# A new order table, a division by exponentials in the first slabs, and a shorter range check placed late, in a linear attention and feed-forward kernel

## The chip, the cores and the metric

The kernel runs on one NeuronCore of a Trainium2 chip. Its engines are TensorE (PE in the profile; PEld is its loading of weights), VectorE (DVE), ScalarE (ACT), GpSimd (POOL) and SyncE (SP, which here only issues DMAs). The metric is the device time of one execution in microseconds (us): three runs of the kernel before gave 621.87, 622.42 and 624.62, median 622.42.

## The reference

Inputs are q, k, v and a complex decay a = a_re + i a_im for 4 batches, 8 heads, 768 time steps and head size 48. The decay is scaled so that its magnitude is at most 0.999. Then the state of each head, a 48 x 48 complex matrix, runs through time, and the result goes into a gated feed-forward layer (384 to 1536 to 384) over 3072 tokens:

```python
for t in range(S):
    new_re = ar * S_re - ai * S_im
    new_im = ar * S_im + ai * S_re
    S_re, S_im = new_re + kv, new_im          # kv = outer(k[t], v[t])
    y[:, :, t] = einsum('bhd,bhde->bhe', q[:, :, t], S_re)
g = x @ w_gate; val = x @ w_val               # x is y with the heads side by side
out = (g / (1 + exp(-g)) * val) @ w_out
```

The weights come as 64-bit floats.

## The kernel before

**The work.** Time is cut into 6 chunks of 128 steps, so 4 batches give 24 slabs (n = 0 to 23) of 128 steps by 8 heads. Two slabs form a group (g = 0 to 11); the names of operations end in the group, or in group.slab, or in the slab. Group 0 is prepared in two halves, 0a and 0b, which are 384 columns wide (8 heads x 48); all others are 768 wide.

**Preparation of a group** (`stage_ops`). The recurrence is replaced by running sums along time of ln|a| and of the angle of a. `ld_re`, `ld_im`, `ld_qt`, `ld_kt` load (L439). `sqr`, `sqi`, `m2` make re^2 + im^2; `lnm`, `w`, `l2` its logarithm, cut at 0.999. The angle is arctan(im/re): in group 0 `rec` is a reciprocal of re on DVE (L461) and `ratio` a product with it (L504); in the others `lnr` and `r0` make 1/re as exp(-ln re) on ACT, `e1` and `b1` multiply re and im by it on DVE and `ratio` corrects it (L506). `RCP = 1` says how many groups take the first way. `at` is the arctan. `cumL` and `cumF` are the running sums, products of PE with a triangle of ones (L541, L544). `exps` turns the first into decays; `sadd`, `rnd`, `frac`, `abs`, `cos`, `sin` turn the second into a phase, and `qtm`, `ktm`, `qs0`, `qs1`, `ks0`, `ks1` scale q and k by both. `dr1`, `dr2` send the decay of the last step through DRAM and back as the small tile `dec`, which `gm` multiplies into the state G (L400).

**A slab** (`slab_ops`). q and k are turned so that heads lie on partitions (tile T): in slabs 0 to 3 by PE (`tr`, L669, copied out by `ev`), later by DVE transposes of 32 x 32 (`tr1`, `tr0`, L689) into a lent weight tile ww, and 12 DMAs that bring the strips into place (`sh0` to `sh3`, L697). `sc` are the scores on PE, `mk` the mask on DVE (L758), `kv` the new state, `st` and `V` the values (L730, L799), `evh` and `evl` copy the result as x into a high and a low part (L817).

**Feed-forward** (`ffn_ops`), 12 steps per group: `f1_g.i` gate and value (L974), `th` Silu on ACT, `h2` the product on DVE (L985), `hh` and `hl` its high and low part, `f2_g.i` the output product (L1005). Six steps of group 0 use whole 32-bit weights (6 products for f1, 3 for f2); in all others each product is split into three of half the precision (18 and 9 products). `oe` and `os` copy out and store.

**Weights.** `wl0` load (L857), `c1` and `c3` build 32-bit floats from 64-bit ones (L869), `c4` and `c5` split them, for w_in (names end in w) and w_out (o). All weights are loaded in the first 60 us.

**Range checks.** The shortcuts hold for a range of inputs only. `kl`, `k1`, `k2` read all weights again and check them (L908, L912, L917); `ckre`, `ckim` check groups 2 to 11. `sector_ops` checks slabs 0, 6, 12 and 18, and their neighbours in groups 0 and 1: two loads, re - im and re + im on DVE (`kz0`, `kz1`), and the smallest of each (`km0`, `km1`, L941). `judge`, `tally`, `keep` (L1032 to L1044) make one count of all flags; if it is not 128, a slow general version runs.

**What sets the order.** All engines work through their own queue in order. The queues are filled from one table, `ORDER`, a list of some 2150 names, each with its engine where there is a choice (`c10w:DVE`). `Planner.plan` walks it, asserts that each name stands behind what it depends on, and puts a table load of ACT (L1103) where the next function isn't in the set that is loaded. A name's place in the list is not a time: only its place among the names of the same engine counts. `tt` (L400) and `cast` (L404, L406) are helpers, so many operations share these lines.

Of the kernel before, what the change touches and what calls it, by code (L numbers as in the profile page):

```python
# [24 lines left out]
NSLAB = B * NCH  # L25
# [9 lines left out]
RCP, SQR = 1, 2  # L35
ORDER = """
    ld_re0a ld_re0b ld_im0a ld_im0b ld_re1 ldv0 ld_im1 ldr0 wl00w wl01w ld_qt0b wl02w ld_kt0a ld_qt0a sqr0a:ACT
    sqi0a:ACT sqr0b:ACT rec0a ratio0a at0a m20a:DVE sqi0b:DVE m20b:DVE cumF0.0 lnm0a lnm0b w0a lnr1 rec0b
    sqr1:ACT sadd0.0:ACT w0b r01 l20a sqi1:DVE m21:DVE cumL0.0 exps0.0 lnm1 w1 c10w:DVE c30w ratio0b rnd0a
    frac0a:DVE c11w:DVE e11:DVE c31w abs0a at0b cumF0.1 wl04w dr10a b11:DVE ratio1 sin0a c12w:ACT cos0a l20b  # L40
    cumL0.1 at1 sadd0.1:ACT exps0.1 l21 cumL1.0 ktm0a:DVE qtm0a:DVE ks0_0a:DVE ks1_0a:DVE qs1_0a:DVE rnd0b
    frac0b:DVE qs0_0a:DVE trt010 exps1.0 wl03w ldr1 wl00o ld_kt0b ld_qt1 wl01o wl05w dr10b ldv1 dr20a trt011
    c32w c13w:DVE cumF1.0 evt010:ACT abs0b evt011:ACT trt000 trt001 sadd1.0:DVE ld_re2 ld_kt1 wl06w c33w
    evt001:DVE qtm0b:DVE c14w:DVE sin0b cumF1.1 sadd1.1:ACT evt000:ACT cumL1.1 cos0b sc0_0 sc1_0 exps1.1
    ktm0b:DVE ks0_0b:DVE ks1_0b:DVE c10o:ACT mk0_0 c34w qs1_0b:DVE qs0_0b:DVE trt110 trt111 evt110:ACT
    evt111:ACT kv0 c15w:ACT trt100 trt101 evt100:ACT evt101:ACT mk1_0 V0 dr11 wl03o dr20b wl02o wl07w fr0b
# [1235 lines left out]
```

## Time and profile before

| | us |
|---|---|
| median of 3 runs | 622.42 |
| the profiled execution | 622.05 |
| its span, first to last instruction | 620.5 |
| PE busy | 587.4 |
| PEld busy | 564.7 |
| DVE busy | 480.2 |
| ACT busy | 383.3 |
| of that, 89 table loads of ACT, 1283 ns each | 114.2 |

Busy times of engines lie beside each other. Matmuls overlap in PE's pipeline and their ends are modelled, so busy PE says little of its pace; the distance from start to start says more. A wait of an engine matters where it reaches the end. Idle time of another engine costs nothing.

### The profile page before, as it was taken

How to read it: one execution, taken by the hardware profiler on the slowest of the kernel's cores; microseconds unless marked ns; L12 is line 12 of the kernel's file. 1: busy time of each engine (PE TensorE's matmuls, PEld its weight loads, DVE VectorE, ACT ScalarE, POOL GpSimd, SP SyncE). 2: the span in 40 equal slices, each digit the busy share in tenths (PEclk: the TensorE clock that was granted, in tenths of full speed). 3: DMA queues.
4: the chain of work that ended last, by engine and by line, in shares of the span. 5: the costliest groups of instructions: out<-in, count | busy, mean ns of one | idle time of the engine just before them, and what ended most of it. 6: DMA issues, size and time to landing. Idle time of an engine off the chain costs nothing.

```text
span 620.5 us, 16959 instructions
## 1 busy us (share of the span) xinstructions
PE 587.4 (95%) x7004; PEld 564.7 (91%) x7004; DVE 480.2 (77%) x885; ACT 383.3 (62%) x668; POOL 5.6 (1%) x17
## 2 busy tenths in 40 slices
PE   2699999999989999999999999999999999999994
PEld 0378899999989999999999999999999999999994
DVE  8999999988868768978768879778766947643332
ACT  7988995864874776666857687556757365311210
POOL 3000000000000000000000000000000000000000
PEclk9999999999999999999999999999999999999999
DMA  8999125455565542664662665645571561133001
GB/s 283 334 338 306 38 48 140 119 150 157 133 173 120 133 109 54 132 161 117 135 162 73 163 157 114 162 125 117 138 173 52 130 188 52 24 101 85 28 1 30
DMA packets 154426, 81.52 MB, mean 131 GB/s; under 512 B 122715, under 2 KB 145501, under 8 KB 154342
## 3 DMA queue, kind: packets, MB, share of 16 engines
q1 hardware_dynamic: 153798, 80.11, 48.5%
q8 instruction: 57, 0.93, 0.7%
q10 hardware_dynamic: 544, 0.26, 0.1%
q14 instruction: 27, 0.22, 0.1%
HBM read 59.82 MB, written 4.78 MB: 104 GB/s over the span
## 4 chain that ended last, share of the span: by engine, by line
PE 69%; DMA 9%; DVE 7%; SPq 7%; ACT 5%; issue 3%; DVEq 0%; ACTq 0%
PE p_gv L974 36%; PE p_po L1005 18%; PE p_py L730 6%; SPq L697 5%; PE p_ps L730 5%; DMA T<-ww 2%; PE p_pm L544 2%; PE p_pm L799 2%; ACT L1103 2%; DVE ww L689 1%; DMA ww<-in_a_im_dram 1%; DMA vt<-in_v_dram 1%; DMA ww<-in_w_in_dram 1%; DMA wo<-in_w_out_dram 1%; ACT s L449 1%
## 5 line engine op out<-in xcount | busy, mean ns | idle before, releaser
L974 PE MATMUL p_gv<-xh,ww 128*128 128x256 f32 x1728 | 316.4, 282 | 1.0 <-ACT xh L817 0.6
L974 PEld LDWEIGHTS p_gv<-xh,ww 128*128 128x128 f32 x1728 | 270.9, 188 | 4.2 <-issue 1.0
L974 PE MATMUL p_gv<-xl,ww 128*128 128x256 f32 x828 | 229.6, 277 | 0.0
L974 PEld LDWEIGHTS p_gv<-xl,ww 128*128 128x128 f32 x828 | 155.5, 188 | 0.0
L1005 PE MATMUL p_po<-hh,wo 128*128 128x256 f32 x828 | 148.5, 279 | 0.0
L1005 PEld LDWEIGHTS p_po<-hh,wo 128*128 128x128 f32 x828 | 126.2, 188 | 2.4 <-issue 2.0
L980 ACT ACTIVATE sg<-p_gv 128x256 f32<-128x256 f32 x144 | 54.4, 383 | 116.6 <-PE p_gv L974 99.6
L1103 ACT ACT_TABLE_LOAD x89 | 114.2, 1283 | 1.6
L1005 PE MATMUL p_po<-hl,wo 128*128 128x256 f32 x414 | 114.8, 277 | 0.0
L985 DVE TENSOR_TENSOR sg<-sg,p_gv 128x256 f32<-128x256 f32 x144 | 59.0, 415 | 46.4 <-ACT sg L980 46.0
L1005 PEld LDWEIGHTS p_po<-hl,wo 128*128 128x128 f32 x414 | 77.7, 188 | 0.0
L400 DVE TENSOR_TENSOR hl<-sg,hh 128x256 fp32r<-128x256 f32 x138 | 57.2, 420 | 11.7 <-ACT hh L404 8.5
L449 ACT ACTIVATE s<-s 128x768 f32<-128x768 f32 x44 | 36.9, 844 | 12.0 <-DVE s L400 7.0
L758 DVE TENSOR_TENSOR sc<-p_ps,turn 128x512 f32<-128x512 f32 x48 | 32.5, 687 | 14.5 <-PE p_ps L730 14.2
L730 PEld LDWEIGHTS p_ps<-T 96*64 96x64 f32 x768 | 36.0, 138 | 7.5 <-issue 2.8
L730 PE MATMUL p_ps<-T 96*64 96x128 f32 (+1 forms) x768 | 39.5, 254 | 3.2 <-DMA T<-ww 2.4
L404 ACT CAST hh<-sg 128x256 fp32r<-128x256 f32 x56 | 22.3, 401 | 23.4 <-DVE sg L985 12.3
L406 DVE CAST hh<-sg 128x256 fp32r<-128x256 f32 x82 | 23.5, 288 | 14.9 <-PE p_po L1005 12.8
L730 PE MATMUL p_py<-sc,vr 128*32 128x128 f32 x384 | 26.0, 273 | 0.0
L730 PE MATMUL p_py<-sc,vt 128*32 128x128 f32 x384 | 25.0, 273 | 0.0
L912 DVE TENSOR_REDUCE flags<-wo 128x1 f32<-128x384 f32 x36 | 19.6, 545 | 6.9 <-DMA wo<-in_w_in_dram 6.9
L817 ACT CAST xh<-p_py 128x384 fp32r<-128x384 f32 x22 | 10.4, 474 | 22.1 <-PE p_py L730 22.1
(133 smaller groups left out, 722.7 us busy)
## 6 DMA issues: line engine op xcount, KB each, us to landing
T<-ww SPq DMA_DIRECT2D x240, 64.0 KB, 2.7
wo<-in_w_in_dram SPq DMA_DIRECT2D x24, 384.0 KB, 3.4
ww<-in_w_in_dram SPq DMA_DIRECT2D x12, 767.8 KB, 7.0
vt<-in_v_dram SPq DMA_DIRECT2D x24, 192.0 KB, 3.9
wo<-in_w_out_dram SPq DMA_DIRECT2D x12, 384.0 KB, 3.7
wo<-in_w_out_dram SPq DMA_DIRECT2D x12, 383.8 KB, 5.1
out_dram<-ost SPq DMA_DIRECT2D x34, 128.0 KB, 3.4
re<-in_a_re_dram SPq DMA_DIRECT2D x11, 384.0 KB
```

The costliest lines, as they stand in the source:

```text
L400: V[e].tensor_tensor(out=out, in0=a, in1=b, op=op)
L404: nc.scalar.copy(out=out, in_=in_)
L406: nc.vector.tensor_copy(out=out, in_=in_)
L449: nc.scalar.activation(out=of(to or dst), in_=of(source), func=func, scale=scale, **kw)
L697: nc.sync.dma_start(out=at_["T", n][32 * j:32 * j + 32].rearrange("p x (g i n) -> p (x g) i n", g=4, i=4)[:, :, i], in_=bt()[32 * i:32 * i ...
L730: nc.tensor.matmul(out=o, lhsT=l, rhs=r, start=opens, stop=closes, tile_position=(0, width * slot), skip_group_check=True)
L758: nc.vector.tensor_tensor(out=s.rearrange("p (r m) t -> p r m t", m=2), in0=scores[qd].rearrange("p (r m) t -> p r m t", m=2), in1=m, op=A ...
L974: nc.tensor.matmul(out=gv[:, i, :], lhsT=l, rhs=r, start=(m == 0), stop=(m == len(mm) - 1))
L980: nc.scalar.activation(out=new("sg", I), in_=at_["gv", I][:, 0:2 * P], func=AF.Silu)
L985: nc.vector.tensor_tensor(out=sg, in0=sg, in1=at_["gv", I][:, 2 * P:4 * P], op=ALU.mult)
L1005: nc.tensor.matmul(out=bank(j), lhsT=weight("o", f, part)[:, j * P:j * P + P], rhs=r, start=pos == 0 and m == 0 and j != 1, stop=pos == NF ...
L1103: nc.scalar.preload_act_table_set(op.load)
```

## The change

1. `RCP` goes from 1 to 0: group 0, too, gets 1/re by `lnr`, `r0`, `e1`, `b1`.
2. The range check of the first slabs takes |im| on ACT (`ka`), one difference re - |im| (`kz`) and one minimum (`km`) in place of two differences and two minima; both loads go into the tile ww, and the tile wo is not needed. Four flags become two.
3. The table `ORDER` is another one throughout.

```diff
-RCP, SQR = 1, 2
+RCP, SQR = 0, 2
 ORDER = """
-    ld_re0a ld_re0b ld_im0a ld_im0b ld_re1 ldv0 ld_im1 ldr0 wl00w wl01w ld_qt0b wl02w ld_kt0a ld_qt0a sqr0a:ACT
+    ld_im0a ld_re0a ld_im1 ld_re1 ld_im0b sqi0a:ACT lnr0a r00a sqr0a:DVE m20a:DVE e10a:DVE b10a:DVE ratio0a
...
-    NFL = 2 * NGRP + NSLAB + 6 * NF
+    NFL = 2 * NGRP - 2 + NSLAB + 6 * NF
...
-        both, parts = [(("wo", x), N) for x in range(2)], [(("ww", x), N) for x in range(2)]
+        parts = [(("ww", x), N) for x in range(2)]
+
         def at(t):
-            return spare("o") if t == "re" else spare("w")[:, A2 * (t == "z"):A2 * (t == "z") + A2]
+            return spare("w")[:, A2 * (t == "im"):A2 * (t == "im") + A2]
...
-        for i, (out_, op) in enumerate((("z", ALU.subtract), ("im", ALU.add))):
-            col = fl_re + g + NGRP * i
-
-            def both_(e, out_=out_, op=op):
-                tt(e, at(out_), at("re"), at("im"), op)
-            pl.add(f"kz{i}{N}", EITHER2, both_, deps=["klre" + N, "klim" + N] + ([f"kz0{N}"] if i else []), use=both + parts)
-
-            def least(e, out_=out_, col=col, i=i):
-                nc.vector.tensor_reduce(out=flags[:, col:col + 1], in_=at(out_), axis=AX.X, op=ALU.min)
-            pl.add(f"km{i}{N}", STT2, least, deps=[f"kz{i}{N}"], use=parts)
+        def size(e):
+            nc.scalar.activation(out=at("im"), in_=at("im"), func=AF.Abs)
+        pl.add("ka" + N, cost(("ACT",), A2), size, deps=["klim" + N], use=parts)
+
+        def room(e):
+            tt(e, at("im"), at("re"), at("im"), ALU.subtract)
+        pl.add("kz" + N, EITHER2, room, deps=["klre" + N, "ka" + N], use=parts)
+
+        def least(e):
+            nc.vector.tensor_reduce(out=flags[:, fl_re + g:fl_re + g + 1], in_=at("im"), axis=AX.X, op=ALU.min)
+        pl.add("km" + N, STT2, least, deps=["kz" + N], use=parts)
```

The first place is DVE's queue at the start, from its first arithmetic on (the decays' preparation of slabs 0 and 1; ww_92 and wo_93 hold re, im and squares of group 0, s the same of group 1). Before:

```order
L461 RECIPROCAL ww_94<-ww_92 128x384
L504 SCALAR_TENSOR_TENSOR ww_92<-ww_92,ww_94 128x384
L400 TENSOR_TENSOR wo_93<-wo_93,ww_94 128x384
L400 TENSOR_TENSOR ww_94<-ww_92 128x384
L400 TENSOR_TENSOR wo_93<-wo_93,ww_94 128x384
L461 RECIPROCAL ww_94<-ww_92 128x384
L513 SCALAR_TENSOR_TENSOR wo_93<-wo_93,ww_94 128x384
L400 TENSOR_TENSOR s_172<-im 128x768
L400 TENSOR_TENSOR s_166<-s_166,s_172 128x768
L406 CAST xl<-ww_138 128x768
L869 SCALAR_TENSOR_TENSOR ww_138<-ww_138,xl 128x768
L504 SCALAR_TENSOR_TENSOR ww_92<-ww_92,ww_94 128x384
```

and now:

```order
L399 TENSOR_TENSOR wo_93<-ww_92 128x384
L399 TENSOR_TENSOR wo_93<-wo_93,ww_94 128x384
L399 TENSOR_TENSOR ww_92<-ww_92,ww_94 128x384 x2
L505 SCALAR_TENSOR_TENSOR ww_92<-ww_92 128x384
L512 SCALAR_TENSOR_TENSOR wo_93<-wo_93,ww_94 128x384
L399 TENSOR_TENSOR s_162<-im 128x768
L399 TENSOR_TENSOR s_164<-re 128x768
L399 TENSOR_TENSOR s_164<-s_164,s_162 128x768
L399 TENSOR_TENSOR wo_93<-ww_92 128x384
L602 TENSOR_SCALAR ww_94<-p_gv 128x384
L399 TENSOR_TENSOR ww_94<-ww_92 128x384
L399 TENSOR_TENSOR wo_93<-wo_93,ww_94 128x384
```

Both reciprocals are gone and products with the exponential stand in their place; squares of group 1 and of half 0a have come to DVE, weights (L869) stand further back. The lines of the kernel after are one less here (L400 is L399).

The second place is DVE's queue where the check of the first slabs stood, in the feed-forward part of group 1, ahead of the first transposes of slab 4. Before:

```order
L985 TENSOR_TENSOR sg<-sg,p_gv 128x256
L400 TENSOR_TENSOR hl<-sg,hh 128x256
L400 TENSOR_TENSOR ww_1084<-wo_1088,ww_1084 128x768
L941 TENSOR_REDUCE flags<-ww_1084 128x1
L400 TENSOR_TENSOR ww_1084<-wo_1088,ww_1084 128x768
L985 TENSOR_TENSOR sg<-sg,p_gv 128x256
L941 TENSOR_REDUCE flags<-ww_1084 128x1
L400 TENSOR_TENSOR hl<-sg,hh 128x256
L689 STREAM_TRANSPOSE ww_1084<-ks 128x4x2x3x32
L689 STREAM_TRANSPOSE ww_1084<-qs 128x4x2x3x32
```

and now:

```order
L399 TENSOR_TENSOR hl<-sg,hh 128x256
L399 TENSOR_TENSOR qs<-qt,s_736 128x16x48
L399 TENSOR_TENSOR ks<-kt,s_736 128x16x48
L399 TENSOR_TENSOR hl<-sg,hh 128x256
L399 TENSOR_TENSOR ww_1221<-ww_146,ww_1221 128x768
L988 TENSOR_TENSOR sg<-sg,p_gv 128x256 x2
L688 STREAM_TRANSPOSE ww_1232<-ks 128x4x2x3x32
L688 STREAM_TRANSPOSE ww_1232<-qs 128x4x2x3x32
```

The four differences and minima on ww_1084 are out of this place (the last two pairs; the first two stand somewhat ahead); in the new order the transposes follow the weights directly, and the check stands in groups 9 and 11.

The third place is the end of DVE's queue, from the last low part (`hl`) through the copies of the output (ost) to the verdict. Before:

```order
L985 TENSOR_TENSOR sg<-sg,p_gv 128x256
L406 CAST hh<-sg 128x256
L400 TENSOR_TENSOR hl<-sg,hh 128x256
L406 COPY ost<-p_po 128x256 x2
L1032 TENSOR_SCALAR good<-flags 128x14
L1032 TENSOR_SCALAR good<-flags 128x10
L1032 TENSOR_SCALAR good<-flags 128x24
L1032 TENSOR_SCALAR good<-flags 128x36 x2
L1033 TENSOR_REDUCE good<-good 128x1
```

and now:

```order
L988 TENSOR_TENSOR sg<-sg,p_gv 128x256
L405 CAST hh<-sg 128x256
L399 TENSOR_TENSOR hl<-sg,hh 128x256
L405 COPY ost<-p_po 128x256 x2
L911 TENSOR_REDUCE flags<-wo_1423 128x1
L1035 TENSOR_SCALAR good<-flags 128x12
L1035 TENSOR_SCALAR good<-flags 128x10
L1035 TENSOR_SCALAR good<-flags 128x24
L1035 TENSOR_SCALAR good<-flags 128x36 x2
L1036 TENSOR_REDUCE good<-good 128x1
```

A last weight check (L911, flags from wo) now stands between the copies of the output and the verdict, and two flags of the first slabs are fewer (128x12 for 128x14).

## Rows read from the trace of the kernel before

**Rows 1.** The page, busy time of each engine, share of the span, instructions.
```profile
PE 587.4 (95%) x7004; PEld 564.7 (91%) x7004; DVE 480.2 (77%) x885; ACT 383.3 (62%) x668; POOL 5.6 (1%) x17
```

**Rows 2.** Stretches: length, busy us of each engine, PEclk, DMA share, GB/s.
```profile
0.00:20.00 20.00, 4.32 (x6) 1.50 (x6) 17.19 (x25) 16.36 (x26) 5.58 (x17) 1.00 0.91 314
20.00:40.00 20.00, 18.12 (x199) 13.01 (x202) 19.79 (x35) 19.52 (x34) 0.00 (x0) 1.00 0.93 294
40.00:60.00 20.00, 18.70 (x133) 16.16 (x122) 19.59 (x29) 15.81 (x23) 0.00 (x0) 1.00 1.00 338
11.00:116.00 105.00, 94.80 (x826) 83.12 (x827) 103.68 (x171) 89.22 (x151) 0.00 (x0) 1.00 0.64 207
40.00:120.00 80.00, 78.00 (x671) 73.12 (x660) 79.08 (x132) 63.95 (x106) 0.00 (x0) 1.00 0.51 154
180.00:200.00 20.00, 17.19 (x252) 16.41 (x251) 16.41 (x28) 9.76 (x19) 0.00 (x0) 1.00 0.62 135
```

**Rows 3.** Timeline of PE: start, us, what, idle before and its releaser.
```profile
40.97 2.87 PE L974 MATMUL p_gv<-xh,ww 128*128 128x256 f32 x12 [0.60 <-ACT xh L817]
...
129.16 1.62 PE L730 MATMUL p_ps<-T 96*64 96x128 f32 x32
```

**Rows 4.** The chain that ended last: start, us, what.
```profile
37.80 1.56 PE p_pm L796 x16
39.36 1.06 PE p_py L730 x32
...
520.48 4.09 PE p_gv L974 x36
```

**Rows 5.** Timeline of DVE.
```profile
3.30 2.55 DVE L461 RECIPROCAL ww<-ww 128x384 f32<-128x384 f32 x1 [0.58 <-DMA ww<-in_a_re_dram]
...
23.17 0.55 DVE L400 TENSOR_TENSOR ks<-wo,ww 128x384 f32<-128x384 f32 x1
23.64 0.55 DVE L400 TENSOR_TENSOR ww<-wo,ww 128x384 f32<-128x384 f32 x1
...
39.73 0.95 DVE L400 TENSOR_TENSOR kt<-kt,qs 128x768 f32<-128x768 f32 x1
40.60 0.95 DVE L400 TENSOR_TENSOR qs<-qt,s 128x768 f32<-128x768 f32 x1
...
116.58 0.38 DVE L400 TENSOR_TENSOR hl<-sg,hh 128x256 fp32r<-128x256 f32 x1
```

**Rows 6.** Timeline of ACT in the opening.
```profile
5.53 0.52 ACT L469 ACTIVATE ww<-ww 128x384 f32<-128x384 f32 x1 [1.71 <-DMA ww<-in_a_im_dram]
...
14.03 0.47 ACT L556 ACTIVATE ww<-p_gv 128x384 f32<-128x384 f32 x1
```

**Rows 7.** Instructions on the tile ww, DVE, 100 to 175 us: ns min/median/max.
```profile
L400 DVE TENSOR_TENSOR ww<-wo,ww x4: 949/952/958, 101.5 to 112.4; 128x768 f32<-128x768 f32 x4
L941 DVE TENSOR_REDUCE flags<-ww x4: 946/946/953, 103.7 to 113.6; 128x1 f32<-128x768 f32 x4
```

**Rows 8.** The chain around slab 1: DMA of dec.
```profile
33.51 2.83 DMA dec<-dr
```

**Rows 9.** Waits on T; waits of 130 to 300 us; landings in the chain.
```profile
PE p_ps L730 <- DMA T<-ww: 2.4, 3, 1.0
...
DVE flags L912 <- DMA wo<-in_w_in_dram: 3.0, 1, 3.0
...
PE p_pm L544 <- DVE s L400: 2.0, 1, 2.0
...
139.56 2.06 DMA T<-ww
...
567.20 2.53 DMA T<-ww
```

**Rows 10.** Timeline of DVE at the end.
```profile
612.07 0.76 DVE L406 COPY ost<-p_po 128x256 f32<-128x256 f32 x2 [0.95 <-PE p_po L1005]
612.75 0.49 DVE L1032 TENSOR_SCALAR good<-flags 128x14 f32<-128x14 f32 x5
```

More of the change, by code (lines that the diff above doesn't have):

```diff
@@ new lines @@
+    ld_im0a ld_re0a ld_im1 ld_re1 ld_im0b sqi0a:ACT lnr0a r00a sqr0a:DVE m20a:DVE e10a:DVE b10a:DVE ratio0a
+    lnm0a w0a ld_re0b ld_kt0a ld_qt0a ld_kt0b wl00w ldr0 wl03w wl01w ld_qt0b wl07w wl00o l20a sqi1:DVE sqr1:DVE
+    m21:DVE sqr0b:DVE at0a cumF0.0 cumL0.0 lnr1 r01 sadd0.0:DVE sqi0b:DVE m20b:DVE e11:DVE lnr0b r00b exps0.0
+    qtm0a:DVE b10b:DVE e10b:DVE ratio0b ktm0a:DVE rnd0a frac0a:DVE lnm0b w0b lnm1 w1 at0b cumF0.1 b11:DVE ratio1
+    l20b abs0a sin0a cos0a at1 l21 c10w:DVE cumL0.1 sadd0.1:ACT c30w ks0_0a:DVE ks1_0a:DVE rnd0b frac0b:DVE
@@ new lines @@
+    exps0.1 cumL1.0 dr10a ldv0 fr0a c11w:DVE qs0_0a:DVE qs1_0a:DVE c31w ktm0b:DVE exps1.0 trt010 cumF1.0 wl02w
+    wl01o ldr1 ldv1 wl05w dr10b wl04w dr20a wl06w abs0b evt010:ACT trt011 sadd1.0:ACT trt000 cumF1.1 evt011:DVE
+    sin0b sadd1.1:ACT trt001 evt000:ACT cumL1.1 evt001:ACT cos0b sc0_0 sc1_0 exps1.1 qtm0b:DVE ks1_0b:DVE
+    c12w:DVE c32w c13w:DVE ks0_0b:DVE c33w qs1_0b:DVE qs0_0b:DVE trt110 trt111 kv0 c10o:ACT evt110:ACT
+    evt111:ACT c14w:ACT mk1_0 mk0_0 trt101 trt100 evt101:ACT evt100:ACT V0 rnd1 gm0 frac1:DVE c34w evh0 abs1
@@ new lines @@
+    cos1 ld_qt1 dr11 sc0_1 sc1_1 kv1 mk0_1 mk1_1 V1 evh1 f1_0.0 f1_0.1 ld_kt1 wl03o wl05o ld_im2 ld_re2 qtm1:DVE
+    c30o c15w:DVE c35w ktm1:DVE ks0_1:DVE sin1 c11o:ACT c16w:ACT c36w ks1_1:DVE wl08w ldr2 th_0.0 h2_0.0
+    c17w:ACT th_0.1 wl02o fr0b wl09w dr21 fr1 dr20b wl010w wl011w wl04o ldv2 c37w qs0_1:DVE trt210 f2_0.0 h2_0.1
+    trt211 evt210:ACT sqr2 c18w:ACT evt211:ACT sqi2 c31o qs1_1:DVE ckre2 c12o:ACT c38w m22:DVE f1_0.2 th_0.2
+    trt200 f2_0.1 wl09o wl011o ldr3 wl07o wl06o wl08o lnr2 evt200:ACT h2_0.2 trt201 c32o f2_0.2 c19w:DVE c39w
@@ L192 @@
+    f2_11.5 th_11.7 h2_11.7 hh_11.6:DVE hl_11.6:DVE f2_11.6 f1_11.9 th_11.8 hh_11.7:DVE kzs1:DVE hl_11.7:DVE
+    h2_11.8 f1_11.10 th_11.9 k235 h2_11.9 kms1 hh_11.8:DVE hl_11.8:DVE f2_11.7 f2_11.8 th_11.10 hh_11.9:DVE
+    h2_11.10 f1_11.11 hh_11.10:DVE hl_11.9:DVE f2_11.9 hl_11.10:DVE f2_11.10 th_11.11 h2_11.11 hh_11.11:DVE
+    hl_11.11:DVE f2_11.11 oe11.2 oe11.0 oe11.1 os11.2 os11.1 os11.0 k135 judge tally keep
 """
```

298 lines of the change are left out of this document (140 added, 158 removed).

## The prediction

> **What bounds the kernel now.** I read the engine totals first: PE is busy 95% of the span, DVE 77% [rows 1]. Then the same by stretches [rows 2]: there the share splits. From 11 to 116 us DVE is busy 103.68 of 105 us, PE only 94.80, and only 4.32 of the first 20. So DVE is the limit up to about 116 us, and PE takes what DVE hands over. Later PE fills its stretches but a few; 180 to 200 us with 17.19 is the worst. Last, two places in PE's timeline: the first gate/value step starts at 40.97, the scores of slab 4 at 129.16 [rows 3]. From its first step on PE has the same work in both kernels, about 551 us: 36 split products go by in 4.09 [rows 4], so a split gate/value step of 18 takes 2.04 and an output step of 9 takes 1.02, and a slab of groups 0 and 1 takes 1.62 + 1.56 + 1.06 = 4.2 [rows 3, 4]. The end is therefore the start of that step, plus 551, plus what PE loses after it, plus the tail. Between 40.97 and 129.16 (88.2 us) the order before gives PE 6 whole steps of some 2.6 (15.6) and 17 split ones (34.7), the output steps at half of that, 6 (7.8) and 13 (13.3), two slabs (8.4) and about 5 of transposes and running sums: 84.8. So about 3.5 to 4 are lost there.
>
> By busy time PE seems to lose only 2.0 from 40 to 120 us (78.00 of 80); its weight loads fill 73.12 [rows 2]. The Trainium skill (Perfetto Trace Analysis, Identifying the Most-Contended Engine) calls matmul busy time a poor measure, since matmuls are pipelined, and asks for weight-load time. By busy time my second term would be 1.0 instead of 2.0 and the forecast 619.0; my count from start to start is nearer to the page.
>
> **The opening.** Both reciprocals leave DVE, 2.55 us each [rows 5]. For them come Ln and Exp of half a group on ACT (0.47 to 0.52 each, as its other 384-column instructions [rows 6]) and, on DVE, two products per half, and squares that ACT made before. From start to start a 384-column instruction takes DVE 0.47 and a 768-column one 0.87 [rows 5]. Ahead of the last mask of slab 1 (`mk1_1`) DVE loses 7 instructions: the reciprocals (2.5 each), c35w (0.87), c30o and a total (0.47 each), c14w and a copy (0.6 each), 8.0. It gains 10: four products, two small squares and a total (0.47 each), a large square (0.87), c12w and a copy (0.6 each), 5.4. Net -2.6: 54 instructions with 31.7 us against 51 with 34.3. ACT's work there falls by about 1.5.
>
> Against it stands a later start. re0a came first and was in at 3.30; now im0a is first and re0a second. The third load came at 5.53 [rows 5, 6], so I put re0a at 4.3 (an estimate between those): DVE starts 1.0 later. I walked the chain with these durations: squares and Ln at 4.3, Exp at 4.8, ratio0a done at 6.9, l20a at 7.3, Arctan behind its table load at 7.8, the first running sum at 8.35. The second now follows at once, since l20a no longer stands behind a second reciprocal, and exps0.0 starts at 12.1 instead of 14.03 [rows 6]. From 13 us on DVE has no gap in this walk; 31.7 us of work and 5.2 of start and gaps put the end of the last mask at 36.9. Then values (1.06 [rows 4]) and the copy to xh (0.5): first step at 38.6, **-2.4**. Bounds: 0 (DVE meets a wait that takes it all) and -2.6 (the net work alone); the walk found no such wait, so I stay near the far end.
>
> The place where one could stand is gm0 on DVE, at 33.4 in the walk. It needs the decays (dec), and behind it in DVE's queue are both masks of slab 1, so V1, xh and the first step wait for it. Before, dec came 2.83 us after its issue [rows 7]. Now about 9.2 MB are issued ahead of it; at 314 and 294 GB/s [rows 2] these are through at 30.1, and with 1 us of transfers that overlap it is in at 31. That leaves 2.4. The Trainium skill (DMA: Bandwidth & Descriptors, Queues, rings and completion order) says that each DMA engine takes descriptors in ring order: by that rule dec cannot pass the weights and the margin is these 2.4; without it, dec would come 2.83 after an issue at about 24 and the margin would be 6.
>
> **DVE's lag, 41 to 129 us.** Step f2_1.4 takes its hl at 116.96 (116.58 + 0.38 [rows 5]). PE, at its own pace from 40.97 with the same durations, would start that step at 114.0: 3.0 lost. Up to this hl the order before has 178 DVE instructions with 111.2 us, the order after 184 with 107.5. What leaves is above all the check of the first slabs, 4 differences and 4 minima of 0.95 [rows 8], 7.2 from start to start. With 5.2 of start and gaps, and the 1.1 by which DVE drifted in before, hl comes at 113.8. PE, which starts at 38.6 and has one more split step (2.04) ahead of f2_1.4, is there at 113.7: the lag is gone. I take **-2.0** of the 3.0, since small losses at changes of product stay; bounds 0 and -4.
>
> **The middle.** Before, PE loses 2.0 at a running sum of group 4: it waits for lim4, which stands in DVE's queue behind a weight check that waited 3.0 for its load; and three waits for transposed strips (T) cost 2.4 [rows 9]. By the counts DVE is now about 7 us further ahead of PE there, which may cover such a wait: bounds 0 and -3.3 (with what followed it), half taken, -1.6. The strips come closer to their scores in the new order: in five slabs (5, 7, 9, 13, 23) the last strip is listed at most one PE step ahead of the scores, before in one. Five waits of the usual 0.8 make 4.0 against 2.4: +1.6, half taken, +0.8. Together **-0.8**, bounds -3.3 and +4. The check itself is now 4 instructions on DVE and 2 on ACT, late, where both have room: nothing. Three more table loads (92 against 89, 1.28 each) lie on ACT, which is busy 383 of 620 [rows 1]: nothing, or 3.9 if that cover were gone.
>
> **The tail.** Before, DVE copies two output parts from 612.07 on and judges at 612.75 [rows 10]; count, branch and end follow in a row. Now part 2 is copied first, which needs the very last matmul (+0.35), and one weight check (0.46) stands between copies and verdict: **+0.8**; bounds 0.4 and 1.
>
> **Sum**, against the profiled execution (622.05, of which 620.5 span): -2.4 - 2.0 - 0.8 + 0.8 = -4.4, so 617.65. That execution lies 0.37 below the median of 622.42; on the median, 618.0.
>
> **Rivals.** (a) The opening gains nothing: dec or a weight comes 2.4 later than I reckon plus the margin, and DVE stands still. For it: DMA is full up to 60 us (0.91, 0.93, 1.00 [rows 2]) and would have to keep up with a faster DVE. Against: from 11 us on DVE hardly waited before. Time: 618.0 + 2.4, and half the second term back: 621.4. With it I count that the order changes nothing, because PE is 95% busy: 622.4; the first 41 us, of which PE needs 14, speak against that. (b) More: PE loses nothing from 41 to 129 (-4 for -2.0) and the middle gives its -3.3: 618.0 - 2.0 - 2.5 = 613.5. For it: DVE is 7 to 9 us further ahead by 130 us. Against: small losses stand in stretches where DVE has time, too. (c) Slower, by the strips. If a late place in the list means that the last strip is only issued when PE stands at the scores, each of the five slabs waits a whole landing, 2.06 to 2.53 [rows 9]: 11.5 in place of +0.8, 628.7. From 1.6 a slab on it decides. For it: a T wait ended last in the chain just after such late landings at 139.56 and 567.20. Against: SyncE runs ahead of the list where its queue is free.
>
> **How the numbers follow.** Forecast 0.50, its own range 615.5 to 620.5; (a) 0.22, 620.5 to 623.5; (b) 0.17, 612 to 615.5; (c) 0.11, 625.5 to 631. Half a percent is 3.1 us, about what a measurement of this kernel can tell from no change, so faster means below 619.3: 0.40 of the forecast and all of (b), 0.57. Slower is (c), 0.10; same is the rest, 0.33. The range leaves out (c) and the lower half of (b): 613.5 to 623.5.
>
> **What would show it.** Right: the first gate/value step at 37.6 to 39.6; no DVE wait over 0.5 between 13 and 38 us; the scores of slab 4, with 3.1 less PE work ahead, at 121 to 123; no wait of PE for lim4; at most 4 us of waits for T; the verdict 1.2 after the last output matmul. Wrong: the first step after 40, or waits for T at slabs 5, 7, 9, 13 and 23.

## The result and the profile after

The changed kernel takes **614.1 us** (median of 4 runs, 613.41 to 615.07) against 623.52 of the kernel before beside it: ratio 0.985, 95% interval 0.982 to 0.988. The forecast was 618.0. The profiled execution took 613.41 with a span of 611.5, 9.0 less than before. The direction came out, and three of the four terms in size, one of these for another reason than mine. The fourth, the middle, was nearly six times as large as I put it.

The engine totals of the changed kernel, as in [rows 1]:

```profile
PE 585.9 (96%) x7004; PEld 565.0 (92%) x7004; DVE 477.0 (78%) x894; ACT 385.9 (63%) x666; POOL 6.0 (1%) x17
```

No engine's busy time changed by more than 3.2 us, and PE has the same 7004 matmuls in both: seen from PE the 9 us are time in which it did not get its next work. The same stretches as in [rows 2] (length, busy us of PE, PEld, DVE, ACT, POOL, PEclk, DMA share, GB/s):

```profile
0.00:20.00 20.00, 5.41 (x8) 2.63 (x9) 17.21 (x33) 17.78 (x29) 6.01 (x17) 1.00 0.92 318
20.00:40.00 20.00, 18.43 (x207) 13.62 (x206) 19.86 (x33) 19.15 (x34) 0.00 (x0) 1.00 0.99 337
40.00:60.00 20.00, 20.00 (x131) 17.91 (x130) 19.54 (x31) 15.92 (x24) 0.00 (x0) 1.00 0.93 281
11.00:116.00 105.00, 96.92 (x865) 87.21 (x866) 103.48 (x178) 87.34 (x149) 0.00 (x0) 1.00 0.63 196
40.00:120.00 80.00, 80.00 (x692) 76.12 (x691) 78.75 (x137) 63.26 (x103) 0.00 (x0) 1.00 0.49 137
180.00:200.00 20.00, 19.16 (x272) 18.57 (x271) 17.76 (x33) 10.26 (x20) 0.00 (x0) 1.00 0.62 146
```

VectorE is as full as before up to 116 us, yet PE does 2.1 more in that stretch; and 180 to 200 us, the worst stretch of before, is 2.0 better. Two places of PE's timeline that answer to [rows 3], the first gate/value step (40.97 before) and the scores of slab 4 (129.16 before):

```profile
38.79 5.46 PE L977 MATMUL p_gv<-xh,ww 128*128 128x256 f32 x24 [0.60 <-ACT xh L816]
...
121.06 0.81 PE L729 MATMUL p_ps<-T 96*64 96x128 f32 x12
```

To see where PE loses time I took its trace from start to start: the distance from the first matmul of one kind of work to the first of the next, less the usual distance of that work (2.04 for a split gate/value step, 1.02 for its output step, 4.17 for a slab, and so on). What is left over is a loss. Added up by parts, all in us:

| kernel | median | ratio to before, 95% | first step at | loss up to 123 us | loss after that | behind the last output step |
|---|---|---|---|---|---|---|
| before | 622.42 | | 40.97 | 4.62 | 15.41 | 1.40 |
| after | 614.10 | 0.985, 0.982 to 0.988 | 38.79 | 1.80 | 10.92 | 2.19 |
| x1 | 619.37 | 0.994, 0.992 to 0.997 | 39.19 | 1.80 | 18.34 | 1.39 |
| x2 | 618.66 | 0.993, 0.991 to 0.994 | 41.26 | 4.59 | 10.37 | 2.19 |
| x3 | 623.78 | 1.001, 0.999 to 1.002 | 41.23 | 4.23 | 16.09 | 1.40 |
| x4 | 617.48 | 0.991, 0.989 to 0.993 | 38.79 | 7.44 | 9.00 | 2.19 |
| x5 | 623.76 | 1.002, 0.999 to 1.005 | 40.35 | 4.58 | 16.19 | 1.40 |
| x6 | 619.08 | 0.994, 0.992 to 0.996 | 38.75 | 1.81 | 15.51 | 2.19 |
| x7 | 616.83 | 0.991, 0.988 to 0.993 | 42.31 | 1.78 | 10.20 | 2.18 |
| x8 | 618.90 | 0.994, 0.992 to 0.996 | 38.81 | 1.80 | 17.58 | 1.39 |
| x9 | 625.14 | 1.005, 1.003 to 1.007 | 41.14 | 4.64 | 15.33 | 1.40 |
| x10 | 615.59 | 0.990, 0.989 to 0.992 | 41.22 | 1.78 | 10.31 | 2.19 |
| x11 | 611.82 | 0.984, 0.982 to 0.986 | 39.90 | 1.81 | 9.22 | 1.40 |
| x12 | 619.63 | 0.995, 0.993 to 0.997 | 41.19 | 4.64 | 11.09 | 1.40 |

The four last columns are of one profiled execution each, the medians of 3 to 12 runs. After against before: -2.18 - 2.82 - 4.49 + 0.79 = -8.70. Two things bound such figures. By the trace itself, PE goes from its first gate/value step to its last output step in 570.22 before and 563.11 after, 7.11 less, where the two loss columns give 7.31; and the product of the verdict starts 8.51 earlier, so 0.4 of the span's 9.0 lies behind it. Differences between these columns are good to about half a us. And the kernel before ran again beside each set of runs, with medians from 622.0 to 623.5: two kernels that did not run beside each other are best compared by their ratios. So the question for the experiments was the middle: what made 15.41 into 10.92?

Its waits, by name. PE at the scores (p_ps, which read the strips T) and at the running sums (p_pm), and VectorE and ScalarE at the weight checks (36 of each), are these in the kernel before (groups of instructions: busy us, mean ns, idle before them and its releaser):

```profile
L730 PE MATMUL p_ps<-T 96*64 96x128 f32 (+1 forms) x768 | 39.5, 254 | 3.2 <-DMA T<-ww 2.4 <-issue 0.8
L544 PE MATMUL p_pm<-s,tri 128*128 128x384 f32 x60 | 18.3, 357 | 2.2 <-DVE s L400 2.0 <-DVE G L400 0.2
...
L912 DVE TENSOR_REDUCE flags<-wo 128x1 f32<-128x384 f32 x36 | 19.6, 545 | 6.9 <-DMA wo<-in_w_in_dram 6.9
L917 ACT ACTIVATE wo<-wo 128x384 f32<-128x384 f32 x36 | 20.2, 561 | 4.3 <-DMA wo<-in_w_in_dram 3.6 <-DMA wo<-in_w_out_dram 0.7
```

and these after:

```profile
L729 PE MATMUL p_ps<-T 96*64 96x128 f32 (+1 forms) x768 | 39.5, 254 | 0.0
L543 PE MATMUL p_pm<-s,tri 128*128 128x384 f32 x60 | 17.7, 349 | 0.0
...
L911 DVE TENSOR_REDUCE flags<-wo 128x1 f32<-128x384 f32 x36 | 19.6, 543 | 0.8 <-DMA wo<-in_w_in_dram 0.8
L916 ACT ACTIVATE wo<-wo 128x384 f32<-128x384 f32 x36 | 20.1, 557 | 8.7 <-DMA wo<-in_w_in_dram 8.5
```

All of them are waits for a transfer that came late, directly or one step removed. PE's two are gone, and VectorE's fell from 6.9 to 0.8. ScalarE's doubled, from 4.3 to 8.7, and yet the kernel is faster: what a wait at a check costs here depends on what stands behind it.

### The profile page after: what moved, and what is told of

It is laid out like the page before. It is cut to its first block, busy times and chain, and to the rows that moved or that the text cites. A ratio compares the mean times of both kernels' runs of the same rounds, so it can differ in the third digit from the quotient of the medians.

```text
span 611.5 us, 16958 instructions
## 1 busy us (share of the span) xinstructions
PE 585.9 (96%) x7004; PEld 565.0 (92%) x7004; DVE 477.0 (78%) x894; ACT 385.9 (63%) x666; POOL 6.0 (1%) x17
## 4 chain that ended last, share of the span: by engine, by line
PE 88%; ACT 5%; DVE 3%; issue 1%; DMA 1%; SPq 1%; DVEq 0%
PE p_gv L977 46%; PE p_po L1008 23%; PE p_py L729 6%; PE p_ps L729 6%; PE p_pm L543 2%; PE p_pm L798 2%; ACT L1106 2%; PE p_gv L668 1%; PE p_pm L795 1%; ACT s L448 1%; ACT ww L448 1%; DMA wo<-in_w_in_dram 1%; DMA ww<-in_a_re_dram 0%; DVE sg L988 0%; ACT sg L983 0%
## 5 line engine op out<-in xcount | busy, mean ns | idle before, releaser
L399 DVE TENSOR_TENSOR hl<-sg,hh 128x256 fp32r<-128x256 f32 x138 | 56.6, 418 | 6.3 <-ACT hh L403 4.0
L916 ACT ACTIVATE wo<-wo 128x384 f32<-128x384 f32 x36 | 20.1, 557 | 8.7 <-DMA wo<-in_w_in_dram 8.5
```

The source lines that it names most:

```text
L399: V[e].tensor_tensor(out=out, in0=a, in1=b, op=op)
L916: nc.scalar.activation(out=high(0), in_=high(1), func=AF.Square, accum_out=flags[:, fl_hi + j:fl_hi + j + 1])
```

## Is it VectorE's lead, or the place of things in the list? (x1, x2, x4, x10)

Two theories. **Lead**: VectorE is further ahead of PE when it comes to the middle (some 7 us by my count), and that covers late loads. **Placement**: the new list has loads, strips and checks elsewhere. I joined the two lists at f1_2.0 (142 us), where both have done nearly the same work, once each way round.

```diff
+ x1: list of the changed kernel up to f1_2.0, then the list of before
+ x2: list of before (RCP = 1, old sector check) up to f1_2.0, then the list of the changed kernel
+ x10: list of before (RCP = 1) up to f1_0.0, then the list of the changed kernel
+ x4: changed kernel, 8 x tensor_reduce over 768 columns of a weight, on DVE between sin2 and hl_1.3
```

x1. 

> The new order up to gate/value step f1_2.0 (about 142 us), then the old order for all that is left; the sector check late, in 4 steps, and no reciprocals. Lead theory (the middle got faster because VectorE is about 7 us further ahead of TensorE when it comes there, so that a late load or strip no longer reaches TensorE): the middle gains all the same, and the old tail has no extra 0.8: 8 to 9 us below the kernel before, no wait of TensorE at lim4 (cumF4.0). Rival, placement (the middle gained because the new list puts strips, weight checks and loads elsewhere there): the losses of before at cumF4.0 (2.2), f1_4.9 (1.2) and f2_10.9 (0.9) come back, 4.5 to 5 below the kernel before.

Measured: 3.8 below before. The loss of 2.3 at cumF4.0 came back although the start is the new one, and that at f1_4.9 too (1.8). But the kernel is spoiled by me: where I had put the late sector check it lost 4.2 between 518 and 526 us. Without those its middle is 14.1, nearer to the old 15.4 than to 10.9; x1 by itself decides little.

x2. 

> The mirror image: the old order with its reciprocals and its early sector check in 8 steps up to f1_2.0, then the new order for all that is left. Lead theory: VectorE comes into the middle as late as before, losses like those of before appear in it, and the new tail costs 0.8: between the time of the kernel before and 1 above it. Placement theory: the middle's 4.8 are gained, less 0.8 for the tail: 4 below the kernel before.

Measured: 4.5 below before, as placement has it. VectorE's lead can be read at slab 5, from the start of its second transpose to its scores on PE. Before:

```profile
128.49 0.93 DVE L689 STREAM_TRANSPOSE ww<-qs 128x768 f32<-128x768 f32 x1
142.08 1.63 PE L730 MATMUL p_ps<-T 96*64 96x128 f32 x32 [0.69 <-DMA T<-ww]
```

and x2:

```profile
128.74 0.94 DVE L688 STREAM_TRANSPOSE ww<-qs 128x768 f32<-128x768 f32 x1
142.14 1.65 PE L729 MATMUL p_ps<-T 96*64 96x128 f32 x32 [0.47 <-DMA T<-ww]
```

That is 13.6 and 13.4; after, it is 15.7 (119.63 and 135.35), so the change gives VectorE 2 us more here, not 7. With the lead of before, x2's middle lost only 10.37. PE's busy time from 120 to 600 us shows it in one row per kernel. Before:

```profile
120.00:600.00 480.00, 474.36 (x6034) 464.85 (x6033) 358.02 (x674) 280.98 (x497) 0.00 (x0) 1.00 0.47 118
```

after:

```profile
120.00:600.00 480.00, 478.78 (x6076) 469.69 (x6075) 358.02 (x681) 284.98 (x501) 0.00 (x0) 1.00 0.48 119
```

and x2, old start and new rest:

```profile
120.00:600.00 480.00, 478.60 (x6078) 469.54 (x6078) 359.54 (x684) 285.45 (x499) 0.00 (x0) 1.00 0.47 118
```

The changed kernel gains 4.4 in this stretch, and x2 gains 4.2 without the lead.

x4. 

> The changed kernel with 8 minima over 768 columns (about 0.95 each, 7.6 in all) put on VectorE between 95 and 112 us, where the old sector check stood; their results are used by nothing. Lead theory: the lag comes back (+2 to 2.6) and so does most of what the middle gained (+2 to 4): 4.5 to 6.5 above the changed kernel. Placement theory: +2 to 2.6 only.

Measured: 3.4 above the changed kernel, between the two numbers, but the parts are clear: +5.6 up to 123 us, more than either theory said, and the middle did not suffer; it lost 9.00, less than without the dead work. On lead this says little: PE was held up almost as long as VectorE, so the lead at slab 5 is still 15.0. What x4 does show is that the new list fills VectorE where the old check stood: 7.6 us of work put there cost 5.6.

x10. 

> The old order with its reciprocals up to the first gate/value step (f1_0.0, 41 us), then the new order for all the rest. If the gain between 41 and 120 us (2.65) lies in the new order of that stretch, TensorE loses about 1.7 there as in the changed kernel, and the time is 2 to 2.5 above the changed kernel and 2.5 below the run with the old start up to 142 us. If that gain came from the earlier opening, TensorE loses about 4.3 there again: 4.5 to 5 above the changed kernel.

Measured: 1.5 above the changed kernel by the medians, 3 by the ratios (the kernel before was 1.5 faster beside x10), and below x2 by 3.1 in the medians, 1.4 by the ratios and 2.7 in the spans of the profiled executions. The loss up to 123 us is 1.78 with the old opening: that gain belongs to the list of that stretch, not to the earlier start. The opening is a sum by itself.

## The sector check alone, and the reciprocals alone (x3, x7)

```diff
- klims0 klres0 kz0s0 kz1s0 km1s0 km0s0 klres1 klims1 kz0s1 km0s1 kz1s1 km1s1   (before, 90 to 114 us)
+ klres0 klims0 kas0 kzs0 kms0 ... klres1 klims1 kas1 kzs1 kms1                 (x3: behind kl33 and os10.1)
```

x3. 

> The kernel before in its own order and with its reciprocals; only the sector check of the first groups is moved to the end of the list and made in 4 steps. Lead theory: 7 us of VectorE's work leave the stretch 100 to 114 us, so the lag there goes (2 to 2.6) and most of the middle's 4.8 too: 5 to 7 below the kernel before. Placement theory: only the lag goes: 2 to 2.6 below.

Measured: no gain, against both theories. VectorE's busy time from 40 to 120 us fell by 6, PE's hardly rose (before 78.00, [rows 2]):

```profile
40.00:120.00 80.00, 78.17 (x678) 73.53 (x671) 73.09 (x126) 64.24 (x107) 0.00 (x0) 1.00 0.45 137
```

The loss up to 123 us went from 4.62 to 4.23 only. The losses of before are not where the check stood, but earlier: 0.90 at the transposes of slab 2 (43.7), 0.98 at slab 2's attention (62.8), 0.46 at slab 3's (77.4); at 100 us only 0.44. After they are 0, 0.28, 0.26 and 0. (x3's middle holds 2.5 at f2_9.8, again at the place that I gave the late check.)

```diff
- RCP, SQR = 0, 2          - lnr0a  r00a e10a b10a      - lnr0b  r00b e10b b10b
+ RCP, SQR = 1, 2          + rec0a                      + rec0b
```

x7. 

> The changed kernel with the two reciprocals of the first group back on VectorE (2.55 each) at the places of the two first Ln, without the two Exp and the four products. My sum for the division part: +5.1 of VectorE's time less six small instructions at 0.47 (2.8): the first gate/value step 2 to 2.6 later than in the changed kernel and the time 2 to 2.6 above it. Rival (the gain of the opening came from the order of the loads and the earlier first running sums): less than 1 above it.

Measured: 2.7 above the changed kernel; first step at 42.31, 3.5 later, and the losses behind it hardly changed (1.78 and 10.20). The division part was worth the whole gain of the opening and more: with the reciprocals the new opening would be 1.3 worse than the old. The sum was 0.9 to 1.5 short; 0.77 of that is a wait that it left out. VectorE stands at l20a (8.57 us) for lnm0a and w0a on ScalarE, which the reciprocal held up; the changed kernel has no wait there.

## What in the list: SyncE's queue (x5, x6, x8, x9, x12)

The worst place of before is cumF4.0. Before, VectorE's check k16 waits for its load, lim4 stands behind it, and PE waits for lim4:

```profile
182.19 0.55 DVE L912 TENSOR_REDUCE flags<-wo 128x1 f32<-128x384 f32 x1 [2.97 <-DMA wo<-in_w_in_dram]
182.66 0.42 DVE L400 TENSOR_TENSOR hl<-sg,hh 128x256 fp32r<-128x256 f32 x1
182.99 0.95 DVE L400 TENSOR_TENSOR s<-im,s 128x768 fp32r<-128x768 f32 x1
```

x5 moves the check, x6 puts the load and the check late in the changed kernel.

```diff
 x5:  exps4.1 k26 th_2.9 evh6
- k16
  hl_2.8:DVE lim4:DVE cumF4.0 qtm4:DVE sadd4.0
+ k16
 x6:
- ldr7 kl6 os1.2 ... h2_2.8 k16 f2_2.7 th_2.9 k26 at4 ... exps4.1 f1_2.10 lim4:DVE
+ ldr7 os1.2 ... h2_2.8 kl6 f2_2.7 th_2.9 at4 ... exps4.1 k16 k26 f1_2.10 lim4:DVE
```

x5. 

> The kernel before with one word of its list moved: weight check k16 on VectorE stands behind qtm4 and sadd4.0 instead of ahead of lim4. By the theory of the queue (cumF4.0 waits for lim4 only because k16 ahead of it waits 2.97 for its load) TensorE's 2.2 at cumF4.0 go, and perhaps the 1.0 at f2_2.9 behind it: 2 to 3 below the kernel before. Rival (lim4 is late by VectorE's own work): nothing changes, within 0.5.

Measured: no gain, and yet neither theory is right. The wait for lim4 is gone (0.2 left at the running sums). But PE, which is 2.6 earlier now, waits 1.44 for the strips of slab 7 a few us later, and its waits for T are 5.3 in this execution instead of 2.4. What was late was not only the check's load; the strips behind it in SyncE's queue were late, too. That gives back only some 0.9 of the 2.2, at slab 7 (1.6 instead of 1.0 ahead of its scores) and just behind it (0.4). Another 1.5 is lost at the scores of slabs 5, 11 and 23, where nothing was moved; slab 5 even stands ahead of the moved word, and cost 0.9 before and 1.5 here. So two executions can differ by that much, and how much the move itself gives back stays open.

x6. 

> The changed kernel with the load kl6 put late (behind h2_2.8) and check k16 just ahead of lim4, as they stood before. VectorE is about 7 us further ahead here than it was before. Queue theory: the load lands when it lands, VectorE stands at it, and cumF4.0 waits about 2 again: 1.5 to 2.5 above the changed kernel. Lead theory: 7 us of lead cover a wait of 3: within 0.5 of the changed kernel.

Measured: 5.0 above the changed kernel (5.7 by the ratios), more than twice what I expected, and by another way. VectorE did not wait at k16. SyncE did: the next check's load (kl5) needs the buffer that check 6 holds until k26 ends on ScalarE, at 178.46. So SyncE stood at it from 171.42 to 178.48, and behind it stood the strips of slab 7:

```profile
171.03 0.39 SPq L907 DMA_DIRECT2D wo<-in_w_in_dram  x1
178.48 0.33 SPq L907 DMA_DIRECT2D wo<-in_w_out_dram  x1
178.87 4.38 SPq L696 DMA_DIRECT2D T<-ww  x6
183.29 0.61 SPq L704 DMA_DIRECT2D vt<-in_v_dram  x1
183.95 1.98 SPq L696 DMA_DIRECT2D T<-ww  x3
```

So x6 says nothing on lim4, and much on the queue. PE waited for the last strip:

```profile
187.74 0.57 PE L729 MATMUL p_ps<-T 96*64 96x128 f32 x5 [4.01 <-DMA T<-ww]
```

x8 was meant as a mending and became the clearest case. I moved `fr4` ahead of ldr8 (four transfers of v), and with it ahead of ldv7 and the last strips of slab 7 (sh1_7):

```diff
- abs4 cos4 ldv7 h2_2.11 sh1_7 ld_re5 dr14 ... evh7 ldr8 ld_im5 fr4 dr24
+ abs4 fr4 cos4 ldv7 h2_2.11 sh1_7 ld_re5 dr14 ... evh7 ldr8 ld_im5 dr24
- hh_2.0:DVE tr1_6 oe1.1:DVE f1_2.1 f1_2.2 oe1.0:ACT k22 th_2.1
+ hh_2.0:DVE oe1.1:DVE tr1_6 f1_2.1 f1_2.2 th_2.1 oe1.0:ACT k22
- f2_11.11 oe11.2 oe11.0 oe11.1 os11.2 os11.1 os11.0 k135 judge
+ hl_11.8:DVE k135 ... f2_11.11 oe11.1 oe11.0 oe11.2 os11.1 os11.2 os11.0 judge
```

x8. 

> The changed kernel with three places of its list mended: the last weight check k135 three steps earlier and the output copies in the old sequence (1.40 instead of 2.19 behind the last product, -0.8); fr4 ahead of the strip loads ldr8 (sin4 waited for it, and f1_3.2 for sin4 by way of h2_3.0: -1.1); th_2.1 ahead of an output copy and k22 on ScalarE (f1_2.3 waited: -0.7). All three: 2.0 to 2.6 below the changed kernel. If the losses only move to the next step: 0.8 below.

Measured: 4.8 above the changed kernel. Two mendings hold (0.79 at the end, 0.37 at f1_2.3). The third cost 7.1: fr4 needs the fraction of group 4, which VectorE finishes at 183.7, and SyncE stood before it from 177.42 on. In SyncE's queue (SPq):

```profile
173.71 3.71 SPq L696 DMA_DIRECT2D T<-ww  x5
183.75 0.26 SPq L621 DMA_DIRECT2D fr<-s  x1
184.05 0.61 SPq L704 DMA_DIRECT2D vt<-in_v_dram  x1
184.70 1.99 SPq L696 DMA_DIRECT2D T<-ww  x3
```

and the scores of slab 7 on PE:

```profile
188.42 0.91 PE L729 MATMUL p_ps<-T 96*64 96x128 f32 x8 [5.20 <-DMA T<-ww]
```

So I took the kernel before and changed only what SyncE's queue holds up. Slab 23 shows the other half of the matter: over the 240 strips of the kernel before, one issue kept SyncE 0.61 us in the median (at least 0.59), a slab has 12 strips, and whatever stands between them comes on top. Before, the strips of slab 23 took 14.0 us from first to last (PE then waited 0.71):

```profile
554.29 1.95 SPq L697 DMA_DIRECT2D T<-ww  x3
556.34 0.61 SPq L705 DMA_DIRECT2D vt<-in_v_dram  x1
557.05 0.60 SPq L908 DMA_DIRECT2D wo<-in_w_in_dram  x1
557.70 2.51 SPq L697 DMA_DIRECT2D T<-ww  x3
560.26 2.69 SPq L719 DMA_DIRECT2D vr<-in_v_dram  x4
562.99 2.23 SPq L697 DMA_DIRECT2D T<-ww  x3
565.26 0.59 SPq L1020 DMA_DIRECT2D out_dram<-ost  x1
565.91 2.37 SPq L697 DMA_DIRECT2D T<-ww  x3
```

after, 8.4:

```profile
545.18 8.44 SPq L696 DMA_DIRECT2D T<-ww  x12
```

```diff
 x9 and x12:
- sh0_5 cy3 ldv5 ... sh2_5 sh1_5 sh3_5
+ sh0_5 cy3 ... sh2_5 sh1_5 sh3_5 ldv5
- frac6:DVE ld_im7 dr16 sh1_11
+ frac6:DVE sh1_11 ld_im7 dr16
- sh0_23 ldv23 kl30 sh3_23 ldr23 sh2_23 os9.2 sh1_23
+ sh0_23 sh3_23 sh2_23 sh1_23 ldv23 kl30 ldr23 os9.2
 x9 only:
- k25 k15 hh_2.7:DVE sc0_6 os1.2 sh0_7 ldv7 kl6
+ k25 k15 kl6 hh_2.7:DVE sc0_6 os1.2 sh0_7 ldv7
 x12 only:
- ldv7 kl6 ... k26 th_2.9 evh6 k16 ... f2_2.8 ld_re5 ldv8 sh1_7
+ ldv7 ... th_2.9 evh6 ... f2_2.8 sh1_7 ld_re5 ldv8 ... k130 k230 kl6 ... k26 ... k16
```

x9. 

> The kernel before with transfers moved in SyncE's queue alone, no engine's work touched: load kl6 goes ahead of the strips of slab 7 (for k16 ahead of lim4); loads that stand between the strips of slabs 5, 11 and 23 (ldv5; ld_im7 and dr16; ldv23, kl30, ldr23 and os9.2) go behind the last strip. Theory: the middle's loss is made by the order in SyncE's queue. Then cumF4.0 (2.2), f2_2.9 (1.0), f1_4.9 (1.2), f2_10.9 (0.9) and most of f2_1.10 (0.9) go: 4.5 to 6 below the kernel before. Rival (the losses are VectorE's and move on): less than 1.5 below.

Measured: 3.1 above before. The three strip moves did what they should: the losses at f2_1.10, f1_4.9 and f2_10.9 are gone, and so is the 2.2 at cumF4.0. But SyncE, with kl6 in front, stood 2.8 us until its buffer was free, and issued the last strips of slab 7 at 185.24 instead of 184.24, while PE, without the wait at lim4, came there 2.5 earlier. Slab 7 paid for it: 3.74 at f2_2.9 and 1.51 in the slab, the sum 15.33 against 15.41. In its profiled execution, the fastest of its six, that made it even; what made the others slower, no trace shows.

x12. 

> The kernel before, again with SyncE's queue changed, but so that no load that must wait for a buffer stands ahead of strips: the loads between the strips of slabs 5, 7, 11 and 23 go behind them (ldv5; ld_re5 and ldv8; ld_im7 and dr16; ldv23, kl30, ldr23 and os9.2), and weight check 6 (kl6, k16, k26) goes as a whole from the stretch at 175 to 182 us to the end, behind k230. Theory (the middle's loss is made where SyncE or VectorE stands at a transfer and strips or lim4 stand behind it): the losses at cumF4.0 (2.2), f2_2.9 (1.0), f2_1.10 (0.9), f1_4.9 (1.2) and f2_10.9 (0.9) all go and none comes back: 5 to 6 below the kernel before. Rival (they are given back at the next step, as in the two kernels that moved k16 or kl6 alone): within 1.5 of the kernel before.

Measured: 2.8 below before, half of what I expected in the median; the profiled execution's middle fell by 4.3 (15.41 to 11.09), nearly all of what the changed kernel gained there. The five places gave 5.8: 2.2 at cumF4.0, where check 6 was taken from VectorE, and 3.5 at the strips. 1.4 came back in small pieces, the largest (0.7 behind f1_3.0) where VectorE now waits 1.9 at the next check, k17. PE's waits for T (before 3.2) and for the running sum (2.2):

```profile
L729 PE MATMUL p_ps<-T 96*64 96x128 f32 (+1 forms) x768 | 39.5, 254 | 0.0
L543 PE MATMUL p_pm<-s,tri 128*128 128x384 f32 x60 | 18.0, 354 | 0.1
```

So the order of SyncE's queue, with one check put late as a whole, is enough for nearly all of the middle's gain. Of the 4.3 the span kept 3.5 (620.5 to 617.0): the first step came 0.2 later and 0.6 more lies behind the verdict. The runs spread over 618.0 to 621.2; why the median gains only 2.8 stays open.

## Two mendings kept and one more place (x11)

The largest loss left in the changed kernel, 1.12 at f1_3.2, is of the same kind: ScalarE waits 2.93 for the load of check 7, and th_3.0 stands behind it. x11 has x8's two good mendings and this one:

```diff
- tr1_8 k27 oe2.0:ACT f1_3.0 f1_3.1 th_3.0 h2_3.0 hh_3.0:ACT th_3.1
+ tr1_8 oe2.0:ACT f1_3.0 f1_3.1 th_3.0 h2_3.0 hh_3.0:ACT th_3.1 k27
```

x11. 

> The changed kernel with fr4 left where it was. Kept from the first mending: k135 three steps earlier with the old sequence of the last copies (-0.8), th_2.1 ahead of an output copy and k22 (-0.4 measured there). New: on ScalarE th_3.0 and th_3.1 stand ahead of k27, which waits 2.9 for its load, so f1_3.2 no longer waits (-1.1). In all 2.0 to 2.4 below the changed kernel, about 612. Rival: the losses move to the next step, 1.2 below.

Measured: 611.82, ratio to before 0.984 against the changed kernel's 0.985, 2.3 below its median but only some 0.6 by the ratios. The intervals overlap, so a gain in time is not shown. The profile shows the losses gone where the list was changed, 1.7 less in the middle and 0.8 less at the end. The span fell by 1.2 only, since this execution's first step came 1.1 later with the same list up to there. By busy time PE is then all but full; the 9.2 that the count still finds behind 123 us stand in pieces of 0.25 at most:

```profile
120.00:600.00 480.00, 479.96 (x6090) 471.33 (x6090) 359.58 (x684) 286.55 (x503) 0.00 (x0) 1.00 0.47 119
```

## Why the prediction was right or wrong

**The opening** (-2.4 forecast, -2.2 measured). Right in size and in its main reason: x7 takes the reciprocals back and loses it, x10 keeps the old opening and loses just that. One execution tells this term only roughly: seven with the old opening reach the first step at 40.35 to 41.26 (median 41.19), six with the new one at 38.75 to 39.90 (median 38.80). The medians give 2.4. The products stand where the walk had them; the first step came at 38.79 (38.6), and VectorE did not wait once between 13 and 38 us. It ran its first square at 3.75 (4.3 estimated):

```profile
3.75 0.56 DVE L399 TENSOR_TENSOR wo<-ww 128x384 f32<-128x384 f32 x1 [1.03 <-DMA ww<-in_a_re_dram]
...
4.89 1.02 DVE L399 TENSOR_TENSOR ww<-ww,ww 128x384 f32<-128x384 f32 x2
...
32.92 0.55 DVE L399 TENSOR_TENSOR G<-p_pm,dec 96x384 f32<-96x384 f32 x1
```

The last row is gm0, the place of rival (a): dec was in time. Whether its margin was 2.4 or 6, as the ring order would decide, no run tells. (In the prediction [rows 7] and [rows 8] have changed places: the 2.83 of dec stands in rows 8, the 0.95 of the check in rows 7.)

**VectorE's lag, 41 to 129** (-2.0; -2.8). The size was nearly right by luck, the reason wrong. I said that what leaves is above all the check of the first slabs. x3 takes away that check alone and gains 0.4 there. The step that failed is the one at f2_1.4: I took its hl, which ends at 116.96, for what PE waited for, and put the 3.0 lost until then down to it. PE comes to f2_1.4 only at 117.41, straight from the product ahead of it. The losses stood at 43 to 78 us, where VectorE had other work in front of what PE wanted. The new list has that work later: the last split of w_out (c50o) stood ahead of f2_0.8 and stands now ahead of f2_1.4, where the check was. x10 shows that the list of this stretch makes the gain, x4 that the room is used. That it is the splits is argued from the list only. The Trainium skill's warning on matmul busy time (Perfetto Trace Analysis, Identifying the Most-Contended Engine) is borne out: from 40 to 120 us busy PE fills all 80.00 after, though the count still finds 1.8 lost; it rose by 2.00, weight loads by 3.00, and the count from start to start says 2.8.

**The middle** (-0.8; -4.5). This is the mis-sized term, and it holds 3.7 of the 4.3 us that the forecast was short. Both its halves failed. (1) I took half of the 3.3 at lim4, because I thought that lead would cover it, perhaps. It went whole, and without lead (x2): in the changed kernel the load is issued 12 us earlier, at 165.49 instead of 177.13, and the running sum that needs lim4 starts only 3 us earlier, at 178.71 instead of 181.70. (2) I gave the strips +0.8, since in five slabs the last strip is listed close to its scores. They gave -2.9 (0.9, 1.2 and 0.9). The distance in the list was the wrong measure. What counts is when SyncE comes to the strip, and that is set by what stands in front of it in SyncE's own queue, above all by a transfer that must wait for a buffer or for VectorE. I named that queue against rival (c) and did not count it. Some of the gain is taken back by losses at new places (1.12 at f1_3.2 above all).

**The tail** (+0.8; +0.79). Right, and mended in x11. The sign held, too: PE's last output product ends at 603.08, and the verdict begins on VectorE at 604.24, 1.2 behind it. PE then waits 2.0 in all for the judged flags, 1.2 before.

```profile
602.80 0.28 PE L1008 MATMUL p_po<-hl,wo 128*128 128x256 f32 x1
...
603.11 0.76 DVE L405 COPY ost<-p_po 128x256 f32<-128x256 f32 x2 [1.30 <-PE p_po L1008]
603.78 0.54 DVE L911 TENSOR_REDUCE flags<-wo 128x1 f32<-128x384 f32 x1
604.24 0.49 DVE L1035 TENSOR_SCALAR good<-flags 128x12 f32<-128x12 f32 x5
```

**The rivals.** (a) did not occur. (b), 613.5, is nearest in size, but its mechanism (VectorE's lead) is refuted by x2. The measured 614.1 lies in its range and not in that of the forecast (615.5 to 620.5); that my whole range held it is luck. (c) did not occur, for T is never waited for; x6, x8 and x9 show that its mechanism is real where SyncE stands.

## What to carry to other kernels

Read a new order queue by queue, the queue that only issues transfers first. For each transfer on which a consumer waits, ask what stands in front of it there and whether that must itself wait for a buffer or a result; the distance in the program did not say it here. When a wait is removed by moving the waiting instruction, look for what else is late behind it, or the loss comes back a few steps on (in part in x5, whole in x9). And test the reason of a term that came out right, too: x3 showed that the lag went for another reason than the one I gave.

## What I had not expected of the hardware

SyncE is a resource of its own: it does not appear in the engine totals, yet 12 strips took it 8.4 us from first to last with nothing in between, and 14.0 with seven other transfers between them. The slab's scores come after that and the landing of the last strip (2.1 us at least over the strips of before, 2.7 in the median). A transfer that must wait holds up what stands behind it in the queue: in x8 SyncE stood 6.3 us before fr4, and PE then waited 5.2 for strips that have nothing to do with it. Executions differ as well: the loss ahead of slab 5's scores was 0.9 before and 1.5 in x5, whose list is the same up to there.
